# Chunked attention with memory slots feeding a Snake MLP: V loads with their edge rows, x blocks by crossbar, and loads moved between phases

## The chip, the cores and the metric

The kernel runs on one core of a Trainium2 chip. The metric is device time in microseconds (us) of one execution. A core has TensorE (PE, matmuls), VectorE (DVE), ScalarE (ACT), GpSimd (POOL) and SyncE (SP), each with an instruction stream of its own that runs in the order of the program. GpSimd and SyncE here mostly issue DMA transfers. "Idle before" of an instruction is the time in which its engine stood still just before it.

## The reference

Four batches, eight heads, 768 positions, head size 64. Each chunk of 32 queries attends to its own 32 keys, 16 to the left, 8 to the right, and to 8 memory keys. The result, put together over the heads, is the x of an MLP.

```python
for c in range(nc):                                   # chunk = 32
    l_start = max(0, c_start - 16)
    r_end = min(S, c_end + 8)
    k_full = concat([mem_k, k[:, :, l_start:r_end]])
    v_full = concat([mem_v, v[:, :, l_start:r_end]])
    scores = scale * matmul(q_c, k_full^T)
    a = exp(scores - max);  a = a / (sum(a) + 1e-09)
    out[:, :, c_start:c_end] = matmul(a, v_full)
x = out.transpose(0, 2, 1, 3).reshape(3072, 512)
h = x @ w_in                                          # 512 -> 2048
s = sin(alpha * h)
g = h + s * s / (alpha + 1e-09)
return g @ w_out                                      # 2048 -> 512
```

## The kernel before

Queries are taken in 8 blocks of 96 (three chunks). A block meets 128 rows of keys and values: rows 0 to 63 and 72 to 127 are positions from 16 before the block to 8 behind it, rows 64 to 71 the memory slots. Rows that a chunk must not see get a bias of -30000 before the exponential. The values tile `vw` has one more column of ones, which yields the sum for the division.

The order is: attention of batch 0 (arranged by pairs of heads, "units" of a pair and half of the blocks); MLP pass 0; attention of batch 1; pass 1; and so on. A pass has 16 tiles of the hidden width: `half_first` makes h in PSUM, ScalarE the sine, one of three engines the square, VectorE the sum g into `gT`. The second product (`second`) of a pass is fed in slices into the phases that follow it, and its output is copied to `o_sb` (two buffers) and stored by SyncE's queue.

Loads of V for a batch: the rows of the block itself in two transfers, the edge rows from the neighbours in two more. In batch 0 the edges come first for all heads, then four pairs of heads.

```python
def load_v(b, parts=((0, H),)):
    vw = vws[b % 2][:].rearrange("p h j c -> p (h j) c")
    vf = v[b].rearrange("h (j t) d -> t (h j) d", t=QW)
    n = H * NJ
    if len(parts) > 1:
        load_v_edges(vw, vf, n)
    for h0, h1 in parts:
        c0, c1 = h0 * NJ, h1 * NJ
        nc.gpsimd.dma_start(vw[16:64, c0:c1, 0:D], vf[0:48, c0:c1])
        nc.gpsimd.dma_start(vw[72:120, c0:c1, 0:D], vf[48:96, c0:c1])
    if len(parts) == 1:
        load_v_edges(vw, vf, n)

def put_memv(b, eng, h0, h1): ...    # memory values of batch 0: one VectorE copy
def send_memv(b):                    # of the others: 8 small transfers
    for j in range(NJ):
        nc.sync.dma_start(vws[b % 2][64:72, :, j, 0:D], memv_st[64:72, b])
```

Batches 2 and 3 get k and q as rows (`load_rows`, GpSimd's queue) and turn them by the crossbar, a DMA that transposes, issued by SyncE:

```python
def cross_steps(b):
    for j in range(NJ):
        nc.sync.dma_start_transpose(kTs[b % 2][:, :, P * j:P * j + P], kst[:, j, :])
        yield
    for t in range(NSUB):
        nc.sync.dma_start_transpose(qTs[b % 2][:, :, P * t:P * t + P], qst[:, t, :])
        yield
```

The attention of batches 1 to 3. A value block `x_blk` (96 queries x 512) reaches xT either by crossbar (`j < crossed`) or by four TensorE transposes and a VectorE copy (`turn_x`):

```python
for s in range(NJ + lag + 1):
    if s < NJ:
        ptl[s] = scores(b, s)
    stream.take(n // 2)              # slices of the second product
    if s >= beside_from:
        next(beside, None)           # a crossbar step of the next batch
    j = s - lag
    if j == NJ:
        ahead(1, 0, xT)              # first half of the MLP's tile 1
    if 0 <= j < NJ:
        xbl[j] = values(b, j, ptl.pop(j))
        if j < crossed:
            nc.sync.dma_start_transpose(xT[:, :, QW * j:QW * j + QW], xbl.pop(j)...)
    stream.take(n - n // 2)
    if j == NJ - 1:
        ahead(0, 0, xT)
    if crossed <= j - 1 < NJ:
        turn_x(xT, j - 1, xbl.pop(j - 1))
```

Attention of batch 0 (`turn_k`, `turn_q`: six transposes of a pair and the copies; `sc`: scores of a pair and two exponentials; `pv`: values of a unit, with a reciprocal and a multiply on VectorE; `x`: turn of a unit and a ScalarE copy; `warm(n)`: n matmuls on zeros that keep TensorE busy):

```python
turn_k(0); warm(2); turn_q(0)
...                                  # memory keys
put_memk(0); warm(3); turn_k(1); warm(2); sc(0); turn_q(1)
alphas()
put_memv(0, nc.vector, 0, H)
warm(2); turn_k(2); warm(2); sc(1); turn_q(2); turn_k(3)
warm(4); turn_q(3); sc(2); warm(2); sc(3)
nc.scalar.preload_act_table(ACTF.Sin)
send_memv(1)
plan(big=(4, 0, 2), one=(6, 7))      # PSUM banks of the next steps
units = [(hp, half) for hp in range(HP - 1) for half in range(2)]
pv(0, 0)
for n in range(1, len(units)):
    warm(1); pv(*units[n]); warm(1); x(*units[n - 1])
warm(1)
pv(3, 0); x(2, 1); pv(3, 1); x(3, 0)
ahead(0, 0, xT); ahead(1, 0, xT); x(3, 1); ahead(2, 0, xT)
```

The passes after the first:

```python
load_rows(2)
crossings = cross_steps(2)
xT = attention(1, feed, (6, 8, 4, 4, 4, 3, 3, 3, 3, 1, 1), 2, 0, crossings, 3)   # 0: none crossed
load_v(2)
send_memv(2)
for i in range(1, B):
    last = i == B - 1
    if i > 1:
        crossings = cross_steps(i + 1) if not last else iter(())
    def begin(ft, i=i):
        if ft == (2 if i > 1 else 0):
            for _ in crossings:
                pass
    if i == 1:
        layer(i, xT, "VAVAVAVAAVAAVAVA", begin, 0)      # the engine of each square
        ...
    else:
        layer(i, xT, "AAAV", begin, feed.left() - (0 if last else 16))
    if not last:
        if i + 2 < B:
            load_rows(i + 2)
        ...
        xT = attention(i + 1, feed, (4, 8, 4, 4, 3, 3, 3, 3, 4, 4, 4), 2, 5 if i == B - 2 else 0)
        if i + 2 < B:
            load_v(i + 2)
            send_memv(i + 2)
```

Of the kernel before, what the change touches and what calls it, by code (L numbers as in the profile page):

```python
# [10 lines left out]
QW = 96  # L11
# [31 lines left out]
def kernel(  # L43
# [12 lines left out]
    nc = tc.nc  # L56
    B, H, S, D = q.shape
# [3 lines left out]
    NJ = S // QW  # L61
    HP = H // 2
# [69 lines left out]
        qb = qkst.tile([P, H, 6, D], BF, name="q_bf")  # L132
        return kb, qb

    def load_rows(b):
        for j in range(NJ):
            lo = QW * j - 16
            r0 = max(0, -lo)
            nc.gpsimd.dma_start(  # L139
                kst[r0:64, j, :].rearrange("p (h d) -> p h d", d=D),  # L140
                k[b, :, lo + r0:lo + 64, :].rearrange("h p d -> p h d"),
            )
            n = min(56, S - (QW * j + 48))
            nc.gpsimd.dma_start(  # L144
                kst[72:72 + n, j, :].rearrange("p (h d) -> p h d", d=D),
                k[b, :, QW * j + 48:QW * j + 48 + n, :].rearrange("h p d -> p h d"),
            )
        nc.sync.dma_start(
            kst[64:72], memk_st[64:72, b - 2, :].unsqueeze(1).to_broadcast([NM, NJ, H * D])
        )  # L150
        for t in range(NSUB):
            nc.gpsimd.dma_start(  # L152
                qst[:, t, :].rearrange("p (h d) -> p h d", d=D),
                q[b, :, P * t:P * t + P, :].rearrange("h p d -> p h d"),
            )
# [15 lines left out]

    def load_v(b, parts=((0, H),)):
        vw = vws[b % 2][:].rearrange("p h j c -> p (h j) c")
        vf = v[b].rearrange("h (j t) d -> t (h j) d", t=QW)
        n = H * NJ
        if len(parts) > 1:
            load_v_edges(vw, vf, n)
        for h0, h1 in parts:
            c0, c1 = h0 * NJ, h1 * NJ
            nc.gpsimd.dma_start(vw[16:64, c0:c1, 0:D], vf[0:48, c0:c1])  # L180
            nc.gpsimd.dma_start(vw[72:120, c0:c1, 0:D], vf[48:96, c0:c1])
        if len(parts) == 1:
            load_v_edges(vw, vf, n)

    def load_v_edges(vw, vf, n):
        nc.gpsimd.dma_start(vw[0:16, 1:n, 0:D], vf[80:96, 0:n - 1])
        nc.gpsimd.dma_start(vw[120:128, 0:n - 1, 0:D], vf[0:8, 1:n])

    def put_memv(b, eng, h0, h1):
        eng.tensor_copy(  # L190
            vws[b % 2][64:72, h0:h1, :, 0:D],
            memv_st[64:72, b, h0:h1, :].unsqueeze(2).to_broadcast([NM, h1 - h0, NJ, D]),
        )

    def send_memv(b):
        for j in range(NJ):
            nc.sync.dma_start(vws[b % 2][64:72, :, j, 0:D], memv_st[64:72, b])
# [122 lines left out]
    def warm(n):  # L320
        z = ps[:, rings["one"][0], :]
        for _ in range(n):
            nc.tensor.matmul(z, idle[:, 0:P], idle[:])  # L323
# [55 lines left out]
    def attention_first(kq, alphas, ahead):  # L379
        xT = xp.tile([P, KT, S], BF, name="xT")  # L380
        pt, xb = {}, {}

        def turn_k(hp):
            t = turn(kq[0], hp, None)
            put_k(0, hp, t)
            put_k_edges(0, hp, t)

        def turn_q(hp):
            put_q(0, hp, turn(kq[1], hp, None))

        def sc(hp):
            for half in range(2):
                pt[hp, half] = unit_scores(hp, half)

        def pv(*u):
            xb[u] = unit_values(*u, pt[u])

        def x(*u):
            unit_turn(xT, *u, xb.pop(u))

        turn_k(0)
        warm(2)
        turn_q(0)
        mt = packed(single(), HP, 32)
        for g in range(HP):
            nc.tensor.transpose(mt[:, g, :], memk_bf[0:32, 2 * g:2 * g + 2, :].rearrange("p e d -> p (e d)"), ident[0:32, 0:32])
        nc.vector.tensor_copy(memkT[:], mt)
        put_memk(0)
        warm(3)
        turn_k(1)  # L410
        warm(2)
        sc(0)
        turn_q(1)
        alphas()
        put_memv(0, nc.vector, 0, H)
        warm(2)
        turn_k(2)
        warm(2)
        sc(1)
        turn_q(2)  # L420
        turn_k(3)
        warm(4)
        turn_q(3)
        sc(2)
        warm(2)
        sc(3)
        nc.scalar.preload_act_table(ACTF.Sin)
        send_memv(1)
        plan(big=(4, 0, 2), one=(6, 7))
        units = [(hp, half) for hp in range(HP - 1) for half in range(2)]  # L430
        pv(0, 0)
        for n in range(1, len(units)):
            warm(1)
            pv(*units[n])
            warm(1)
            x(*units[n - 1])
        warm(1)
        pv(3, 0)
        x(2, 1)
        pv(3, 1)  # L440
        x(3, 0)
        ahead(0, 0, xT)
        ahead(1, 0, xT)
        x(3, 1)
        ahead(2, 0, xT)
        return xT
# [73 lines left out]
    def second(i, gT, cut=0):  # L520

        def begin_o():
            bank = take_bank("one")
            kept.add(bank)
            return bank

        def part(s, bank, f0, f1):
            for ft in range(f0, f1):
                nc.tensor.matmul(  # L529
                    ps[:, bank, :], gT[:, ft, P * s:P * s + P], w_out_sb[:, ft, :],  # L530
                    start=(ft == 0), stop=(ft == FT - 1),
                )
                if ft < FT - 1:
                    yield

        def end_o(s, bank):
            kept.remove(bank)
            rings["one"].remove(bank)
            rings["one"].append(bank)
            o_sb = mlp.tile([P, d_model], F32, name="o_sb", bufs=2)  # L540
            if s % 2 == 0 and not state["attending"]:
                nc.vector.tensor_copy(o_sb[:], ps[:, bank, :])  # L542
            else:
                nc.scalar.copy(o_sb[:], ps[:, bank, :])  # L544
            nc.sync.dma_start(out[S * i + P * s:S * i + P * s + P, :], o_sb[:])

        early = []
        if cut:
            for s in range(2):
                early.append(begin_o())  # L550
                yield from part(s, early[s], 0, cut)
        for s in range(NSUB):
            bank = early[s] if s < len(early) else begin_o()
            yield from part(s, bank, cut if s < len(early) else 0, FT)
            end_o(s, bank)
            yield
# [15 lines left out]
        nc.vector.memset(vw[96:128, H - 1, NJ - 1, 0:D], 0.0)  # L572
    load_qk(0, kq, 0, 2)
    masks.make_identity(nc, ident[:])
    for hp in range(1, HP):
        load_qk(0, kq, 2 * hp, 2 * hp + 2)
    load_v(0, [(2 * hp, 2 * hp + 2) for hp in range(HP)])
    nc.gpsimd.dma_start(memv_st[64:72, 1:B].rearrange("n b h d -> n (b h) d"),
                        mem_v[1:B].rearrange("b h n d -> n (b h) d"))
    for kT in kTs:  # L580
        nc.vector.memset(kT[:, :, 0:16], 0.0)
        nc.vector.memset(kT[:, :, 848:856], 0.0)
# [37 lines left out]
    xT = attention_first(kq, alphas, ahead)  # L620
    for c in range(2):
        load_w_out(c)
    kq1 = alloc_qk()
    load_qk(1, kq1, 0, H)
    for bb in range(2):
# [29 lines left out]
    def begin_0(ft):  # L655
        if ft == 3:
            plan(h=[6] + rings["big"])
        if ft == 11:
            load_v(1)
        if ft == 15:  # L660
            prs.extend(pair_up(kq1[0], n) for n in range(3))

# [15 lines left out]
        feed.take(2)  # L678
    nc.scalar.preload_act_table(ACTF.Exp)
    feed.take(4)  # L680
    load_rows(2)
    crossings = cross_steps(2)
    xT = attention(1, feed, (6, 8, 4, 4, 4, 3, 3, 3, 3, 1, 1), 2, 0, crossings, 3)
    load_v(2)
    send_memv(2)

    for i in range(1, B):
        last = i == B - 1
        if i > 1:
            crossings = cross_steps(i + 1) if not last else iter(())  # L690

        def begin(ft, i=i):
            if ft == (2 if i > 1 else 0):
                for _ in crossings:
                    pass

        if i == 1:
            assert feed.left() == 16
            plan(h=[min(rings["one"])] + rings["big"])
            layer(i, xT, "VAVAVAVAAVAAVAVA", begin, 0)  # L700
            free = rings["h"]
            plan(one=(free[0], free[0] + 1), h=free[1:])
        else:
            plan(h=rings["big"])
            layer(i, xT, "AAAV", begin, feed.left() - (0 if last else 16))
        if not last:
            if i + 2 < B:
                load_rows(i + 2)
            plan(big=rings["h"])
            nc.scalar.preload_act_table(ACTF.Exp)  # L710
            feed.take(6)
            xT = attention(i + 1, feed, (4, 8, 4, 4, 3, 3, 3, 3, 4, 4, 4), 2, 5 if i == B - 2 else 0)
            if i + 2 < B:
                load_v(i + 2)
                send_memv(i + 2)
    feed.take(200)


# [28 lines left out]
```

The softmax here doesn't subtract the row's maximum and nothing guards it: scores larger than these inputs give would overflow.

## Time and profile before

| | |
|---|---|
| time, median of 3 runs | 226.51 us (226.2 to 227.45) |
| profiled span | 226.2 us |
| granted clock of TensorE | full throughout |
| loads on GpSimd's queue | 71520 packets, 14.81 MB |
| transfers on SyncE's queue | 23032 packets, 10.88 MB |
| matmul of the first MLP product, 128x384 | 512 of them, 326 ns each |
| matmul of the second, 128x512 | 362 in the trace (a few records are missing), 379 ns each |

The durations of matmuls overlap: eight of the first product follow each other in 1.30 us. The profile's page gives busy time by engine, the span in 40 slices (a digit is tenths of the slice), the chain of work that ended last, and groups of instructions by line. L483 is the first product, L529 the second, L503 the sine, L510 and L507 the squares, L513 the sum g, L270 the scores, L296 the values, L313 and L316 the turn of x and its copy, L542 and L544 the output copies, L545 the store, L159 and L162 the crossbar steps of k and q, L467 that of x.

### The profile page before, as it was taken

Reading aid. Unit: us, or ns where it says so; the run is one execution under the profiler, and the core shown is the slowest. Engines: PE = TensorE matmul, PEld = TensorE weight load, DVE = VectorE, ACT = ScalarE, POOL = GpSimd, SP = SyncE. Lnnn points to the kernel's source line nnn. Section 1 sums busy time; section 2 is a strip of 40 time slices with the busy share of each in tenths; the row PEclk is TensorE's granted clock in tenths of the full one; section 3 lists DMA queues with packets and bytes.
Section 4 is the critical chain, followed back from the end, with each engine's and each line's share of the span. In section 5 each row is a group of like instructions: output and inputs, shape, how many; then the busy total and the mean of one; then the engine's idle time right before and its main releaser. Section 6 shows DMA issues by size and latency. Waiting matters only on the chain.

```text
span 226.2 us, 4432 instructions
## 1 busy us (share of the span) xinstructions
PE 212.5 (94%) x1694; PEld 115.9 (51%) x1720; DVE 132.9 (59%) x234; ACT 152.6 (67%) x226; POOL 84.4 (37%) x106
## 2 busy tenths in 40 slices
PE   7998999999998999999999999978999999999992
PEld 2555555555545655554665555534565555544440
DVE  5684748793516769994763875626653773771110
ACT  2558478894787589999756879777939678651011
POOL 8967843796989941185780000000000000000000
PEclk9999999999999999999999999999999999999999
DMA  5999999999999999999999954542330110111211
GB/s 81 174 121 127 157 210 207 206 204 142 103 216 159 142 112 167 117 135 121 151 180 95 96 95 93 96 139 93 73 110 0 49 46 0 48 48 49 93 65 74
DMA packets 94573, 25.97 MB, mean 115 GB/s; under 512 B 82632, under 2 KB 91480, under 8 KB 94552
## 3 DMA queue, kind: packets, MB, share of 16 engines
q0 software_dynamic: 71520, 14.81, 111.5%
q1 hardware_dynamic: 23032, 10.88, 24.5%
q8 instruction: 13, 0.21, 0.5%
q14 instruction: 8, 0.07, 0.1%
HBM read 29.67 MB, written 6.29 MB: 159 GB/s over the span
## 4 chain that ended last, share of the span: by engine, by line
PE 50%; DVE 7%; ACT 4%; SPq 3%; issue 3%; DMA 1%; DVEq 0%; ACTq 0%
PE ps L529 26%; PE ps L483 18%; DVE gT L513 5%; SPq L162 3%; PE ps L296 2%; PE ps L270 2%; DVE u L510 2%; ACT u L503 2%; PE ps L313 1%; ACT u L507 1%; DMA out_dram<-o_sb 1%; ACT o_sb L544 1%; ACT pt L283 0%; DVE o_sb L542 0%; DVEq L513 0%
## 5 line engine op out<-in xcount | busy, mean ns | idle before, releaser
L529 PE MATMUL ps<-w_out_sb,gT 128*128 128x512 bf16 x362 | 94.7, 379 | 1.5 <-ACT o_sb L544 0.4
L483 PE MATMUL ps<-xT,w_in_sb 128*128 128x384 bf16 x512 | 91.2, 326 | 1.6 <-DVE gT L513 1.2
L513 DVE SCALAR_TENSOR_TENSOR gT<-u,inv_alpha,ps 128x768 bf16<-128x768 f32 x64 | 63.3, 1011 | 24.0 <-ACT u L507 20.0
L483 PEld LDWEIGHTS <-w_in_sb 128*128 128x128 bf16 x512 | 49.6, 98 | 39.0 <-issue 3.4
L503 ACT ACTIVATE u<-ps,alpha_sb 128x768 f32<-128x768 f32 x64 | 56.7, 896 | 18.4 <-PE ps L483 17.5
L529 PEld LDWEIGHTS <-gT 128*128 128x128 bf16 x384 | 34.3, 98 | 30.9 <-issue 0.9
L507 ACT ACTIVATE u<-u 128x768 f32<-128x768 f32 x40 | 33.7, 843 | 1.2
L283 ACT ACTIVATE pt<-ps,biasm 128x256 bf16<-128x256 f32 x72 | 28.6, 481 | 6.7 <-PE ps L270 3.2
L544 ACT COPY o_sb<-ps 128x512 f32<-128x512 f32 x16 | 9.4, 589 | 25.5 <-PE ps L529 25.5
L510 DVE TENSOR_TENSOR u<-u 128x768 f32<-128x768 f32 x18 | 17.1, 953 | 6.0 <-ACT u L503 6.0
L542 DVE COPY o_sb<-ps 128x512 f32<-128x512 f32 x8 | 5.5, 690 | 21.8 <-PE ps L529 17.2
L303 DVE TENSOR_TENSOR x_blk<-ps,rinv 96x512 bf16<-96x512 f32 x24 | 16.5, 686 | 0.8
L144 POOL DMA_DIRECT2D kst<-in_k_dram x16 | 11.6, 725 | 8.8 <-DMA vw<-in_v_dram 4.1
L302 DVE RECIPROCAL rinv<-ps 96x8 f32<-96x8 f32 x24 | 4.9, 202 | 17.0 <-ACT pt L283 10.7
L139 POOL DMA_DIRECT2D kst<-in_k_dram x16 | 11.0, 689 | 8.6 <-DMA vw<-in_v_dram 6.2
L323 PE MATMUL ps<-idle 128*128 128x512 bf16 x35 | 12.5, 448 | 1.5 <-DVE vw L571 1.2
L249 ACT COPY kT<-ps 128x672 bf16<-128x672 bf16 x8 | 5.8, 719 | 9.5 <-PE ps L234 6.7
L296 PEld LDWEIGHTS <-pt 128*128 128x128 bf16 x192 | 9.0, 98 | 4.6 <-issue 0.7
L510 POOL TENSOR_TENSOR u<-u 128x768 f32<-128x768 f32 x6 | 8.9, 1495 | 6.1 <-ACT u L503 6.1
L152 POOL DMA_DIRECT2D qst<-in_q_dram x12 | 10.6, 899 | 1.2 <-DMA kst<-in_k_dram 1.2
L270 PE MATMUL ps<-qT,kT 64*128 64x96 bf16 x192 | 8.3, 205 | 2.6 <-DVE gT L513 2.3
L296 PE MATMUL ps<-vw,pt 128*128 128x65 bf16 x192 | 9.8, 193 | 0.4 <-issue 0.3
(77 smaller groups left out, 150.8 us busy)
## 6 DMA issues: line engine op xcount, KB each, us to landing
out_dram<-o_sb SPq DMA_DIRECT2D x24, 256.0 KB
vw<-in_v_dram POOLq DMA_DIRECT2D x6, 384.0 KB, 14.9
w_out_sb<-in_moe_w_out_dram POOLq DMA_DIRECT2D x2, 1024.0 KB, 18.8
w_in_sb<-in_moe_w_in_dram POOLq DMA_DIRECT2D x3, 512.0 KB, 10.1
qst<-in_q_dram POOLq DMA_DIRECT2D x12, 128.0 KB, 7.0
kst<-in_k_dram POOLq DMA_DIRECT2D x14, 64.0 KB, 6.7
kst<-in_k_dram POOLq DMA_DIRECT2D x14, 56.0 KB, 6.4
k_bf<-in_k_dram POOLq DMA_DIRECT2D x4, 192.0 KB, 4.7
```

Source lines behind the costliest of these rows:

```text
L270: nc.tensor.matmul(sc[:, e, QW * hp:QW * hp + QW], kTs[b % 2][64 * e:64 * e + 64, hp, pitch * j:pitch * j + P], qTs[b % 2][64 * e:64 * e + ...
L283: nc.scalar.activation(pt[:, 0:H * QW].rearrange("p (g e c) -> p g e c", g=2, e=4)[:, :, :, 32 * m:32 * m + 32], sc[:, :, 0:4 * QW].rearra ...
L296: nc.tensor.matmul(otv[:, e, hp, :], pt[:, QW * i:QW * i + P], vws[b % 2][:, 2 * hp + e, j, 0:D + 1],)
L303: nc.vector.tensor_tensor(out=x_blk[:].rearrange("p g e d -> p e g d"), in0=otv[0:QW, :, :, 0:D], in1=rinv[:].unsqueeze(3).to_broadcast([Q ...
L323: nc.tensor.matmul(z, idle[:, 0:P], idle[:])
L483: nc.tensor.matmul(hT[:, hf, 0:HALF], w_in_sb[:, kt, P * ft:P * ft + P], xT[:, kt, HALF * hf:HALF * hf + HALF], start=(kt == 0), stop=(kt ...
L503: nc.scalar.activation(u[:], hT[:, :, 0:HALF], ACTF.Sin, scale=alpha_sb[:, ft:ft + 1])
L507: nc.scalar.activation(u[:], u[:], ACTF.Square)
L510: eng.tensor_tensor(out=u[:], in0=u[:], in1=u[:], op=ALU.mult)
L513: nc.vector.scalar_tensor_tensor(out=gT[:, ft, :].rearrange("p (e c) -> p e c", e=2), in0=u[:], scalar=inv_alpha[:, ft:ft + 1], in1=hT[:, ...
L529: nc.tensor.matmul(ps[:, bank, :], gT[:, ft, P * s:P * s + P], w_out_sb[:, ft, :], start=(ft == 0), stop=(ft == FT - 1),)
L544: nc.scalar.copy(o_sb[:], ps[:, bank, :])
```

## The change

V of a block comes in two transfers that hold the edge rows: rows 0 to 63 start 16 positions ahead of the block, rows 72 to 127 run 8 beyond it. What a block takes from the neighbouring head at an end is masked by the bias as before. In batch 0 the transfers of pair 0 are issued right behind k and q of pair 1, and the two units of pair 0 are done amid the scores. In the attentions of batches 1 and 2 five value blocks go by crossbar, as they did in batch 3 only. The crossbar steps of batch 2's k and q move from the attention of batch 1 to pass 1, those of batch 3 are spread over pass 2, one per tile. Row loads of batch 3 move from behind pass 1 to ahead of pass 2, V of batch 3 to pass 1, and the memory values of batches 1 and 2 to pass 0. Squares of pass 1 go to three engines instead of two, and the output copies during an attention all to VectorE.

```diff
@@ load_v (load_v_edges is gone)
+        flat = v.rearrange("b h s d -> (b h s) d")
+        def part(p0, p1, first, c0, c1):
+            r0 = S * H * b + QW * c0 + first
+            nc.gpsimd.dma_start(
+                vw[p0:p1, c0:c1, 0:D],
+                flat[r0:r0 + QW * (c1 - c0)].rearrange("(n t) d -> t n d", t=QW)[0:p1 - p0],
+            )
         for h0, h1 in parts:
             c0, c1 = h0 * NJ, h1 * NJ
+            if b == 0 and h0 == 0:
+                part(16, 64, 0, 0, 1)
+                c0 = 1
+            part(0, 64, -16, c0, c1)
...
+            part(72, 128, 48, c0, c1)
...
@@ attention_first
         turn_k(1)
+        put_memv(0, nc.vector, 0, H)
         warm(2)
         sc(0)
         turn_q(1)
         alphas()
-        put_memv(0, nc.vector, 0, H)
-        warm(2)
+        warm(3)
+        sc(1)
+        pv(0, 0)
+        warm(1)
+        pv(0, 1)
         turn_k(2)
         warm(2)
-        sc(1)
+        x(0, 0)
         turn_q(2)
+        warm(2)
+        x(0, 1)
         turn_k(3)
-        warm(4)
+        warm(1)
+        sc(2)
         turn_q(3)
-        sc(2)
-        warm(2)
+        warm(3)
         sc(3)
         nc.scalar.preload_act_table(ACTF.Sin)
-        send_memv(1)
...
-        units = [(hp, half) for hp in range(HP - 1) for half in range(2)]
-        pv(0, 0)
+        units = [(hp, half) for hp in range(1, HP - 1) for half in range(2)]
+        pv(1, 0)
@@ second
-            if s % 2 == 0 and not state["attending"]:
+            if s % 2 == 0 or state["attending"]:
                 nc.vector.tensor_copy(o_sb[:], ps[:, bank, :])
@@ loads at the start
-    for hp in range(1, HP):
-        load_qk(0, kq, 2 * hp, 2 * hp + 2)
-    load_v(0, [(2 * hp, 2 * hp + 2) for hp in range(HP)])
-    nc.gpsimd.dma_start(memv_st...)              # now behind the loads of w_out
+    load_qk(0, kq, 2, 4)
+    load_v(0, ((0, 2),))
+    load_qk(0, kq, 4, 6)
+    load_qk(0, kq, 6, 8)
+    load_v(0, ((2, 4), (4, 6), (6, 8)))
@@ pass 0
         if ft == 11:
             load_v(1)
+            send_memv(1)
+            send_memv(2)
@@ from batch 1 on
-    load_rows(2)
+    load_k_rows(2)
+    xT = attention(1, feed, (6, 8, 4, 4, 4, 3, 3, 3, 3, 1, 1), 2, 5)
+    load_q_rows(2)
+    load_v(2)
+
     crossings = cross_steps(2)
-    xT = attention(1, feed, (6, 8, 4, 4, 4, 3, 3, 3, 3, 1, 1), 2, 0, crossings, 3)
-    load_v(2)
-    send_memv(2)
...
         def begin(ft, i=i):
-            if ft == (2 if i > 1 else 0):
+            if i == 1:
                 for _ in crossings:
                     pass
+                if ft == 13:
+                    load_v(3)
+            elif i == 2:
+                next(crossings, None)
 
         if i == 1:
-            layer(i, xT, "VAVAVAVAAVAAVAVA", begin, 0)
+            layer(i, xT, "VAVAAVPAAVPAPVAA", begin, 0)
...
+            if i == 2:
+                load_k_rows(3)
+                load_q_rows(3)
+                crossings = cross_steps(3)
             layer(i, xT, "AAAV", begin, feed.left() - (0 if last else 16))
...
-            if i + 2 < B:
-                load_rows(i + 2)
...
-            xT = attention(i + 1, feed, (4, 8, 4, 4, 3, 3, 3, 3, 4, 4, 4), 2, 5 if i == B - 2 else 0)
-            if i + 2 < B:
-                load_v(i + 2)
-                send_memv(i + 2)
+            xT = attention(i + 1, feed, (4, 8, 4, 4, 3, 3, 3, 3, 4, 4, 4), 2, 5)
+            if i == 1:
+                send_memv(3)
```

## The prediction

> **What bounds the kernel now.** I read the page first (busy shares, the 40 slices), then a table of busy time by stage, then the chain of waits inside the two stages that lose most, then groups and DMA landings.
>
> From the page, busy time and the 40 slices:
>
> ```profile
> PE 212.5 (94%) x1694; PEld 115.9 (51%) x1720; DVE 132.9 (59%) x234; ACT 152.6 (67%) x226; POOL 84.4 (37%) x106
> ...
> PE   7998999999998999999999999978999999999992
> DMA  5999999999999999999999954542330110111211
> ```
>
> TensorE works 94% of the span, so a large gain is not to be had: it has to come out of its 13.7 us of idle time or out of the matmuls it is given. Some 1.2 us of the idle time lie at the start and 4.1 at the end (21.46 busy of the 25.60 from 200.6 us on), where nothing is changed. The DMA engines are loaded in the first 23 slices, up to 130 us.
>
> Busy time by stage (columns: stretch, its length, then busy us and instructions of each engine):
>
> ```profile
> 5.64:19.50 13.86, 13.33 (x196) 7.01 (x198) 8.42 (x27) 8.24 (x12) 10.66 (x14) 1.00 2.51 144
> 19.50:28.40 8.90, 7.90 (x114) 5.22 (x116) 6.78 (x16) 5.33 (x9) 7.92 (x11) 1.00 1.78 146
> ...
> 62.00:79.00 17.00, 15.98 (x201) 9.46 (x203) 9.25 (x24) 12.64 (x29) 15.78 (x21) 1.00 1.91 172
> 79.00:102.50 23.50, 22.30 (x134) 12.40 (x134) 20.72 (x23) 21.68 (x26) 9.42 (x14) 1.00 2.29 132
> 102.50:119.00 16.50, 15.78 (x198) 9.53 (x201) 9.93 (x25) 12.34 (x29) 11.95 (x14) 1.00 2.43 151
> ...
> 138.00:153.20 15.20, 13.05 (x80) 6.82 (x82) 7.70 (x9) 11.53 (x16) 0.00 (x0) 1.00 0.52 114
> ```
>
> In order: scores of batch 0, its values, attention of batch 1, MLP pass 1, attention of batch 2, end of MLP pass 2. Pass 1 is the only stage where VectorE (20.72) and ScalarE (21.68) are nearly as full as TensorE; the end of pass 2 is the only one after the start and before the tail with over 2 us of TensorE idle. The chain of waits in these two, 79 to 103 us and 136 to 154 us:
>
> ```profile
> by line: DVE gT L513 30.1%; PE ps L483 21.1%; DVE u L510 18.7%; issue 12.9%; ACT u L503 11.3%; ACT u L507 3.6%; PE ps L270 1.4%; PE ps L529 1.3%; DVEq L513 0.4%
> ```
>
> ```profile
> 147.82 1.22 SPq L162
> ...
> 149.13 2.23 DMA out_dram<-o_sb
> ...
> 151.44 0.69 DVE o_sb L542
> 152.14 0.93 DVE gT L513
> ...
> 153.11 0.35 PE ps L270 x8
> ```
>
> Pass 1 is paced by VectorE (49% of its chain). Pass 2 ends in a queue: 14 crossbar transposes stand in a row on SyncE's queue from 128.97 to 149.03, the output stores wait behind them, VectorE waits 4.60 us for an output buffer, gT comes late, and the scores wait 2.05 us for the bank.
>
> **What the Trainium skill says.** "DMA: Bandwidth & Descriptors", DMA Transpose (X-bar): a plain transpose is issued by SyncE or ScalarE only. So here the transposes share SyncE's order with stores and memory values, as the chain above shows. The same page, Queues, rings and completion order: each DMA engine takes turns between its queues by packets. The trace agrees that they share: the seven transposes of k rows stand on SyncE's queue from 70.93 to 82.95, 1.72 us each, against 1.20 (median) for the five of x blocks (96 rows rather than 128) from 157 us on, when no GpSimd load runs. "GPSIMD Engine Reference", Engine selection, puts a two-input elementwise operation at about twice VectorE's time; here the square takes 1495 ns on GpSimd and 953 on VectorE, 1.6 times. "TensorE: Matmul & The Clock Gate", Measured speedup vs the span model, says matmuls run strictly in order; so TensorE pays in full when the half of x that comes next isn't there.
>
> **The change part by part.**
>
> Start. The V loads of pair 0 are issued at 9.28 and 10.01 now and land 9.4 us later, at 19.4; the first values matmul waits for them at 19.57. Behind q1 (lands 4.11 + 4.4 = 8.5) they should land about 11 (estimate: 120 rows x 16 blocks = 1920 packets, at the rate at which all 7656 V packets of the batch land now between 13.5 and 23.6, 2.5 us). q and k of pairs 2 and 3 come some 2.5 us later, at 12.6 to 16, and aren't needed before. Two of eight values units move into the score stage. After them the phase of values is six units of 0.20 + 0.69 us on VectorE, spaced 0.91 (eight took 20.01 to 27.33). But the score stage grows. Replaying TensorE's order with its durations (idle-filling matmul 0.21, turn of six 0.45, scores of a pair 1.40, x turn 0.18): sc(1) runs to about 13.0, pv(0,1) must wait for the second exponential (14.1) that frees its bank and ends at 14.4, and what follows up to sc(3) is 4 x 0.45 + 8 x 0.21 + 2 x 0.18 + 2 x 1.40 = 6.6: end at 21.1, against 19.34 now. Then 21.5 + 6 x 0.91 = 27.0 against 27.33. **Gain 0.3 us**, not 1.8: what was idle-filling work was partly cover for ScalarE's exponentials.
>
> Five x blocks by crossbar, in batches 1 and 2. Each saves four transposes on TensorE, 0.17 us in the chain where they are packed, and a 0.35 us copy on VectorE. 2 x 5 x 0.17 = **1.7 us**.
>
> Output copies in attention all to VectorE. ScalarE's late copies stopped TensorE for 0.61 us at 70.4 and 0.38 at 111.4 (a transpose and a matmul of the second product waiting for a bank). VectorE has room: 9.25 of 17.00 busy, and five copies less. **Gain 1.0 us**.
>
> Squares of pass 1: seven on VectorE and nine on ScalarE become five, eight, and three on GpSimd. VectorE: 16 x 1.01 + 7 x 0.95 = 22.8 becomes 20.9. ScalarE: 16 x 0.90 + 9 x 0.84 = 22.0 becomes 21.1. TensorE needs 128 x 0.162 = 20.8. The three come level, so not all of 1.9 is won: **1.3 us**.
>
> Transposes of batch 3 one per tile of pass 2 rather than in two blocks. A tile lasts 1.95 us and a transpose 1.3, so the queue of SyncE drains and stores slip in. The 2.05 us wait goes, with 0.2 of smaller ones around it: **2.2 us**. Row loads of batch 3 go behind V, and GpSimd has 20 us for them.
>
> The memory values of batches 1 and 2 go to pass 0 (16 issues of 0.8 to 1.1 us, as now, 45 to 61 us), when SyncE has nothing else, and are off the path. V in two loads of 64 and 56 rows rather than four has the same bytes.
>
> On the other side: crossing x costs latency where loads run. At 62 to 79 and 98 to 115 us GpSimd's queue is full, and a transpose at 1.7 us per 1.3 us step falls behind: five blocks lag by about 2 us plus landing, while the first MLP matmuls of a pass come some 5 us after block 3's values. I allow **0.5 us for each of the two stages**.
>
> Sum: 0.3 + 1.7 + 1.0 + 1.3 + 2.2 - 1.0 = 5.5; 226.5 - 5.5 = 221.0 us.
>
> **The rivals.**
> One: crossing under load becomes the wait. For it: 1.72 against 1.20 us, and TensorE can't go round. Against it: at 158 us crossing has five steps of slack, and SyncE has less else to do in attention after the change (k rows go to pass 1). If each block took 3 us, the half of x would be 3 to 4 us late in both batches: 225 to 228.
> Two: GpSimd's squares stand behind the loads of V. For it: GpSimd waited 5.02 and 4.05 us for V landings in pass 1, and its order is kept. Against it: those waits stood before row loads of batch 3, which move to pass 2; what stands ahead of the first square issues without waiting now (75.37 to 79.6), and the first square comes some 8 us into the pass. If it happened, the 1.3 would be lost and 1 or 2 more: 222 to 224.
> Three: the start gets slower. If ScalarE's table load and exponentials push the last values to 28.5, 1.2 us go: 222.5.
> Four: pass 1 becomes TensorE's and the queue stays clear, without late x: 219.
>
> **Range and chances.** The five gains stand on waits that the trace shows; their sum without the allowance is 6.5 (220.0), with the second or third rival 222 to 224, with the first 225 or more. Range 218.4 to 224.3. 2% is 222.0, 1.0 above my number: faster by over 2% 0.63, within 2% 0.32, slower 0.05 (only the first rival in both batches).
>
> **What would show it.** First values matmul near 13.5 and the last VectorE multiply of batch 0 near 27; no VectorE output copy waiting for a store, and no hole at 147 to 153 (shifted); pass 1 from 23.5 to about 22 us with GpSimd squares of 1.5 us; attention of batches 1 and 2 about 1 us shorter each, without waits of the MLP's first matmul for a crossing of x. It is wrong if that matmul waits for x over 1 us, if GpSimd's squares start later than ScalarE's sine by more than 1 us, or if V of batch 2 lands after its first values matmul.

## The result, and the profile after

The changed kernel takes 234.97 us (median of 4 runs, 234.33 to 235.41) against 226.35 for the kernel before on the same chip: a ratio of 1.037, with a 95% interval of 1.0326 to 1.0415. It is 3.7% slower. The prediction was 221.0, with a range up to 224.3.

The head of the page and three rows of the 40 slices, kernel after:

```profile
span 233.4 us, 4347 instructions
...
PE 212.5 (91%) x1652; PEld 114.3 (49%) x1678; DVE 135.2 (58%) x231; ACT 147.5 (63%) x216; POOL 86.6 (37%) x103
...
PE   7989899989999098999994999999999999999993
PEclk9999999999999859999999999999999999999999
DMA  6999999999999999549999995553321101102212
```

TensorE has 42 instructions fewer and the same busy time: matmuls at a lower clock have eaten what was saved. There are two new holes: slice 14 (75.9 to 81.7 us, digit 0), in which the granted clock falls to 8, and to 5 in the slice behind it; and slice 22 (digit 4), where the clock stays full. Both are named by one row of the waits (total us, times, longest), and both stand at the first matmul of an MLP pass in the timeline of TensorE (start, us, what; in brackets the idle time before it and its releaser), kernel after. The second profile of the kernel before, shown last, has no such wait:

```profile
PE ps L498 <- DMA xT<-x_blk: 9.3, 2, 5.9
```

```profile
75.21 0.38 PE L544 MATMUL ps<-w_out_sb,gT 128*128 128x512 bf16 x1
81.47 1.44 PE L498 MATMUL ps<-xT,w_in_sb 128*128 128x384 bf16 x4 [5.88 <-DMA xT<-x_blk]
...
85.05 4.88 PE L498 MATMUL ps<-xT,w_in_sb 128*128 128x384 bf16 x24
...
125.89 0.81 PE L498 MATMUL ps<-xT,w_in_sb 128*128 128x384 bf16 x4 [3.38 <-DMA xT<-x_blk]
```

```profile
76.41 0.81 PE L483 MATMUL ps<-xT,w_in_sb 128*128 128x384 bf16 x4
```

(L498 is the first product of the MLP, L483 in the kernel before; L544 the second, before L529; L513 is now L528.) The wait is for the crossed x blocks. The first matmul of a pass reads half of x, blocks 0 to 3. The chain of waits, 60 to 95 us, and SyncE's timeline, kernel after, show for how long block 3 was under way:

```profile
73.15 8.18 DMA xT<-x_blk
81.33 0.14 issue
81.47 1.44 PE ps L498 x4
```

```profile
73.15 2.94 SPq L482 DMA_TRANSPOSE xT<-x_blk  x2
```

SyncE begins to issue the crossbar transpose of block 3 (96 rows) at 73.15 us; an issue takes some 1.3 us here. The data is there 8.18 us after that start. This time, from the start of the issue until the data is there, is called the landing below. In batch 2 the landing of block 3 takes 7.17 us (118.59 on).

The rest of the loss is found by dividing the span at the same events in each kernel. The table gives the length of each stage in us, from the starts in the timelines (the last row runs to the end of the last first product); "before, again" is a second profile of the unchanged kernel, for a reason that comes below, and "no crossing" is the changed kernel without the crossing in batches 1 and 2 (an experiment).

| stage | before, again | after | no crossing |
|---|---|---|---|
| start to first product of pass 0 | 26.64 | 26.71 | 26.71 |
| to its second product at the end | 22.51 | 23.09 | 22.99 |
| to first scores of batch 1 | 12.11 | 12.12 | 12.11 |
| attention of batch 1 | 15.15 | 19.55 | 14.64 |
| MLP pass 1 | 24.57 | 27.16 | 25.01 |
| attention of batch 2 | 15.29 | 17.26 | 15.44 |
| MLP pass 2 | 33.40 | 33.42 | 33.42 |
| attention of batch 3 | 13.94 | 13.72 | 13.73 |
| pass 3 to the last tile | 34.72 | 34.69 | 34.68 |

After against no crossing: 4.91 + 2.15 + 1.82 = 8.88 of the 8.9 us between their spans (233.4 and 224.5). So the loss lies in three stages and hangs on the five x blocks.

### The profile page after: what moved, and what is told of

Read it like the earlier page. It is cut to its first block, busy times and chain, and to the rows that moved or that the text cites. A ratio compares the mean times of both kernels' runs of the same rounds, so it can differ in the third digit from the quotient of the medians.

```text
span 233.4 us, 4347 instructions
## 1 busy us (share of the span) xinstructions
PE 212.5 (91%) x1652; PEld 114.3 (49%) x1678; DVE 135.2 (58%) x231; ACT 147.5 (63%) x216; POOL 86.6 (37%) x103
## 4 chain that ended last, share of the span: by engine, by line
PE 69%; DVE 11%; DMA 7%; ACT 6%; issue 5%; POOL 1%; DVEq 0%; ACTq 0%; POOLq 0%
PE ps L544 33%; PE ps L498 26%; DMA xT<-x_blk 7%; DVE gT L528 4%; ACT u L518 3%; PE ps L280 3%; DVE u L525 2%; PE ps L306 2%; DVE qT L266 1%; PE ps L333 1%; PE ps L241 1%; PE ps L244 1%; ACT u L522 1%; PE ps L323 1%; DVE x_blk L372 1%
## 5 line engine op out<-in xcount | busy, mean ns | idle before, releaser
L498 PE MATMUL ps<-xT,w_in_sb 128*128 128x384 bf16 x512 | 93.1, 331 | 10.6 <-DMA xT<-x_blk 9.3
L544 PE MATMUL ps<-w_out_sb,gT 128*128 128x512 bf16 x362 | 94.7, 380 | 2.2 <-DVE gT L528 1.3
L528 DVE SCALAR_TENSOR_TENSOR gT<-u,inv_alpha,ps 128x768 bf16<-128x768 f32 x64 | 63.3, 1012 | 23.8 <-ACT u L522 19.6
L498 PEld LDWEIGHTS <-w_in_sb 128*128 128x128 bf16 x512 | 50.1, 99 | 49.2 <-issue 14.5
L544 PEld LDWEIGHTS <-gT 128*128 128x128 bf16 x384 | 34.4, 98 | 32.5 <-issue 2.1
L522 ACT ACTIVATE u<-u 128x768 f32<-128x768 f32 x39 | 32.9, 843 | 1.2
L557 DVE COPY o_sb<-ps 128x512 f32<-128x512 f32 x17 | 11.7, 689 | 26.9 <-PE ps L544 25.4
L525 POOL TENSOR_TENSOR u<-u 128x768 f32<-128x768 f32 x9 | 13.4, 1501 | 29.9 <-ACT u L518 29.9
L525 DVE TENSOR_TENSOR u<-u 128x768 f32<-128x768 f32 x16 | 16.1, 1004 | 6.8 <-ACT u L518 6.8
L180 POOL DMA_DIRECT2D vw<-in_v_dram x15 | 18.2, 1223 | 0.0
L559 ACT COPY o_sb<-ps 128x512 f32<-128x512 f32 x7 | 4.1, 584 | 19.0 <-PE ps L544 19.0
L333 PE MATMUL ps<-idle 128*128 128x512 bf16 x33 | 11.4, 445 | 1.5 <-DVE vw L586 1.2
L280 PEld LDWEIGHTS <-kT 64*128 64x128 bf16 x192 | 4.8, 94 | 10.2 <-issue 10.2
```

What stands on the lines that cost most here:

```text
L180: nc.gpsimd.dma_start(vw[p0:p1, c0:c1, 0:D], flat[r0:r0 + QW * (c1 - c0)].rearrange("(n t) d -> t n d", t=QW)[0:p1 - p0],)
L280: nc.tensor.matmul(sc[:, e, QW * hp:QW * hp + QW], kTs[b % 2][64 * e:64 * e + 64, hp, pitch * j:pitch * j + P], qTs[b % 2][64 * e:64 * e + ...
L498: nc.tensor.matmul(hT[:, hf, 0:HALF], w_in_sb[:, kt, P * ft:P * ft + P], xT[:, kt, HALF * hf:HALF * hf + HALF], start=(kt == 0), stop=(kt ...
L522: nc.scalar.activation(u[:], u[:], ACTF.Square)
L525: eng.tensor_tensor(out=u[:], in0=u[:], in1=u[:], op=ALU.mult)
L528: nc.vector.scalar_tensor_tensor(out=gT[:, ft, :].rearrange("p (e c) -> p e c", e=2), in0=u[:], scalar=inv_alpha[:, ft:ft + 1], in1=hT[:, ...
```

## The experiments

The leading theory, L: crossing x is late because the transposes share the DMA engines with the loads that GpSimd has in flight then (k and q rows and V of the next batch). Its rival, S: it is late because SyncE's queue also carries output stores, so that a transpose stands behind or beside them. A third question was whether the 2.15 us of pass 1 are a clock lowered by the idle time, or the changed split of squares. No kernel here leaves out any of the computation; a few add a little to it.

### Without the crossing in batches 1 and 2

```diff
-    xT = attention(1, feed, (6, 8, 4, ...), 2, 5)
+    xT = attention(1, feed, (6, 8, 4, ...), 2, 0)
-            xT = attention(i + 1, feed, (...), 2, 5)
+            xT = attention(i + 1, feed, (...), 2, 5 if i == B - 2 else 0)
```

> The changed kernel with one part undone: no x block of batches 1 and 2 goes by crossbar, all are turned on TensorE. Theory L and theory S both say that the crossings cost the stall of the first MLP matmul (5.88 and 3.38 us) and, behind the first of them, about 2.5 us of slowed clock; without them these 11.8 us go, the 2 x 0.85 us of saved transposes come back: about 224.5 us, ratio 0.985 to 0.995 to the kernel before. Theory C (the loss is in other parts, the crossing wait only shows it): above 230 us.

Measured: 226.75 us, ratio 1.0009 (0.9995 to 1.0024). The timeline of TensorE, no crossing:

```profile
76.45 0.81 PE L498 MATMUL ps<-xT,w_in_sb 128*128 128x384 bf16 x4
...
86.17 13.39 PE L498 MATMUL ps<-xT,w_in_sb 128*128 128x384 bf16 x80 [0.15 <-DVE gT L528]
...
100.07 1.46 PE L544 MATMUL ps<-w_out_sb,gT 128*128 128x512 bf16 x6 [0.51 <-DVE gT L528]
...
112.00 0.38 PE L544 MATMUL ps<-w_out_sb,gT 128*128 128x512 bf16 x1 [0.80 <-DVE o_sb L557]
```

The first matmul of the pass waits for nothing. The whole loss is the crossing of these two batches; and all the other parts of the change together, for which the prediction counted 4.8 us, bring nothing that can be measured.

### The loads out of the way, or the stores out of the queue

Loads later: k rows, q rows and V of batch 2 are issued at tile 1 of pass 1, those of batch 3 at tile 1 of pass 2, each held back by a GpSimd square at tile 0; the crossbar steps of k and q follow from tile 2 on. Attention then has crossings and stores but no GpSimd loads.

```diff
-    load_k_rows(2)              # before attention of batch 1
-    load_q_rows(2); load_v(2)   # after it
+                if ft == 1:     # in pass 1; the same for batch 3 in pass 2
+                    load_k_rows(2); load_q_rows(2); load_v(2)
-            layer(i, xT, "VAVAAVPAAVPAPVAA", begin, 0)
+            layer(i, xT, "PAVAAVPAAVPAPVAA", begin, 0)
```

> The changed kernel with crossings kept, but GpSimd's row loads of batch 2 and V of batch 2 held back to pass 1 (behind a GpSimd square of its tile 0), rows and V of batch 3 to pass 2, so that no load runs beside the attentions of batches 1 and 2. Theory L (the loads take the DMA engines' turns): the waits of the first MLP matmul for x, 5.88 and 3.38 us, both fall below 0.5 us, five crossings move in about 7 us, and the clock isn't slowed there. Theory S (output stores in the same queue): they stay at 5 to 6 and 3 to 4 us. The total is not the point, as batch 2's k and q come late for its scores: some 5 to 8 us are lost there.

Stores elsewhere: the output stores of the attention stages go out from ScalarE's queue.

```diff
-            nc.sync.dma_start(out[...], o_sb[:])
+            (nc.scalar if state["attending"] else nc.sync).dma_start(out[...], o_sb[:])
```

> The changed kernel with the output stores of the attentions issued from ScalarE's queue instead of SyncE's, so that only crossings stand in SyncE's. Theory S: waits for x fall from 5.88 and 3.38 us to below 2 and 1, the total to about 226 us. Theory L: the stores still share the engines, waits stay above 4 and 2.5 us, total 231 to 236 us.

Busy time by stage (length, then busy us and instructions of PE, PEld, DVE, ACT, POOL; granted clock; DMA share; GB/s) in the attention of batch 1, first the kernel after, then the one with loads later:

```profile
62.00:76.00 14.00, 13.33 (x168) 6.83 (x171) 7.90 (x19) 11.67 (x26) 13.75 (x18) 1.00 1.90 168
```

```profile
62.00:76.00 14.00, 14.00 (x174) 6.92 (x172) 7.42 (x17) 11.99 (x27) 0.00 (x0) 1.00 0.27 81
```

Timeline of TensorE and chain of waits, loads later:

```profile
76.34 0.81 PE L498 MATMUL ps<-xT,w_in_sb 128*128 128x384 bf16 x4 [0.24 <-DMA xT<-x_blk]
...
130.90 0.81 PE L498 MATMUL ps<-xT,w_in_sb 128*128 128x384 bf16 x4
```

```profile
73.89 2.31 DMA xT<-x_blk
```

Timeline of TensorE, stores elsewhere:

```profile
80.15 1.44 PE L498 MATMUL ps<-xT,w_in_sb 128*128 128x384 bf16 x4 [4.72 <-DMA xT<-x_blk]
...
128.38 1.44 PE L498 MATMUL ps<-xT,w_in_sb 128*128 128x384 bf16 x4 [3.76 <-DMA xT<-x_blk]
```

Without GpSimd's loads (POOL busy 0.00 in place of 13.75, DMA share 0.27 in place of 1.90) the same step takes 2.31 us in place of 8.18, and the waits of 5.88 and 3.38 us become 0.24 and none. With the stores gone from the queue, all five transposes issue in one row (7.56 us from 67.70), and the waits are still 4.72 and 3.76. L stands. S alone does not make the wait: with loads later the stores are still in SyncE's queue, and the wait is gone. Moving them took 1.2 us off one wait and nothing off the other; that is no clean measure of S, since the k transposes of batch 2 then start right behind x, at 75.36 us in place of 86.13. What L leaves open is whether the bytes, the number of small packets or the sharing inside the DMA engines is at fault: rows and V were moved together.

Both kernels are slower as wholes than the changed one, for other reasons than x: loads later takes 250.19 us (1.1041, 1.0987 to 1.1095), because the loads that now stand ahead of GpSimd's squares hold them up (gT waits 24.1 us in total for them, 12.86 before one matmul); stores elsewhere takes 242.22 (1.0686, 1.0643 to 1.0728), with the sine on ScalarE standing still twice behind ScalarE's own stores, 12.77 us up to 88.26 and 11.65 up to 135.40. In the chain of waits the first of these stores is held until a k transpose has landed, at 87.80.

### The clock after the idle time

In the wait of batch 1, TensorE gets 27 matmuls on zeros into a bank that is free; nothing reads them.

```diff
+                if b == 1:
+                    spare = next(n for n in rings["one"] if n not in kept)
+                    for _ in range(27):
+                        nc.tensor.matmul(ps[:, spare, :], idle[:, 0:P], idle[:])
```

> The changed kernel with 27 more matmuls on zeros (27 x 0.213 = 5.75 us) put into TensorE's order ahead of the first MLP matmul of batch 1, that is into the 5.88 us in which it waits for x. If the stall also costs a slowed clock afterwards (24 matmuls in 4.88 us instead of 4.07, four in 1.44 instead of 0.81), the full clock is kept and 2 to 2.5 us are won: 232.6 us. If the slow matmuls come from elsewhere (late x, waits for banks): 235 us as before, or more.

Timeline of TensorE and the row of the granted clock, filled wait:

```profile
76.52 5.99 PE L490 MATMUL ps<-idle 128*128 128x512 bf16 x27 [0.23 <-DVE xT L326]
82.34 0.81 PE L502 MATMUL ps<-xT,w_in_sb 128*128 128x384 bf16 x4
```

```profile
PEclk9999999999999999999999999999999999999999
```

Pass 1 takes 25.01 us, exactly as without the crossing, in place of 27.16: the 2.15 us were the clock that followed the idle time, and not the split of squares. How long an idle stretch must be for this, the runs do not settle. Four matmuls behind the wait take 1.44 us after 5.88 (kernel after) and after 4.72 and 3.76 (stores elsewhere), but 0.81, at full clock, after 3.38 (kernel after) and also after 3.76 in batch 2 of the filled wait. The time is 234.61 us (1.0361, 1.0311 to 1.0412): the total does not show the gain clearly. In this profile the start, which the filling cannot reach, took 0.84 us longer and the two attentions 0.56 more together, which gives most of it back.

### Two blocks in place of five

```diff
-    xT = attention(1, feed, (6, 8, 4, ...), 2, 5)
+    xT = attention(1, feed, (6, 8, 4, ...), 2, 2)
-            xT = attention(i + 1, feed, (...), 2, 5)
+            xT = attention(i + 1, feed, (...), 2, 5 if i == B - 2 else 2)
```

> The changed kernel with two crossed blocks in batches 1 and 2 instead of five (batch 3 keeps five). Theory L with a queue that falls behind (about 2.3 us per block against a step of 1.3 to 1.5): two blocks land some 4 to 5 us after the first is issued, ahead of the first MLP matmul: waits below 0.5 us, and 2 x 2 x 0.17 us of saved transposes: 226.0 us. A theory in which each crossing has a fixed long latency of 8 us (as block 3's): the wait stays at 2 to 4 us, 230 us or more.

Measured: 224.99 us, 0.9952 (0.9933 to 0.9972). The pass begins at 75.86 without a wait; attention of batch 1 takes 14.03 us. Blocks 0 and 1 cross at 67.84 to 71.3 and have over 4 us to land; the later blocks do not. A fixed landing of 8 us is ruled out. The stage is 0.61 us shorter than without the crossing, where 0.34 was expected; why stays open.

### The kernel before, looked at again

The queue at the end of pass 2, for which the prediction counted 2.2 us, stood in one profile only. A second one of the unchanged kernel:

> The kernel before, unchanged, profiled once more: the first profile has a span of 226.2 us, while its runs lie around 224.8 us of span. If the 2.05 us wait of the scores for gT at 153 us belongs to every execution, it is there again and the term of 2.2 us stands; then the missing 2 us of the run without crossings are lost elsewhere. If the first profile caught an unusually long queue, the wait is below 1 us now and the term was too large from the start.

Timeline of TensorE, kernel before, second profile:

```profile
149.67 0.34 PE L270 MATMUL ps<-qT,kT 64*128 64x96 bf16 x8
150.91 0.34 PE L270 MATMUL ps<-qT,kT 64*128 64x96 bf16 x8
```

No wait stands before the scores, where the first profile has one of 2.05 us. Its span is 224.0 us and the first profile's 226.2: the prediction had read an execution that was longer than most. In this one the crossings of q ended at 146.6 in place of 149.0, and four stores followed at once. Most of the 2.2 us was not there to win.

### The squares of pass 1

Old split, without the crossing of x in batches 1 and 2, so that nothing on GpSimd but loads runs in pass 1:

```diff
-            layer(i, xT, "VAVAAVPAAVPAPVAA", begin, 0)
+            layer(i, xT, "VAVAVAVAAVAAVAVA", begin, 0)
```

> The kernel without crossings of batches 1 and 2 and, besides, with the squares of pass 1 as before (seven on VectorE, nine on ScalarE, none on GpSimd). If my term of 1.3 us for the squares holds: 1.3 us longer than without crossings alone, 228.0 us. If what its trace shows is right (0.4 us won in the stream of matmuls, 0.4 lost at the end of the pass, where V loads of batch 3 stand on GpSimd): within 0.5 us of it, 226.8 to 227.3 us.

Timelines of GpSimd and of TensorE, old split:

```profile
85.38 1.72 POOL L180 DMA_DIRECT2D vw<-in_v_dram  x1 [5.04 <-issue]
```

```profile
102.96 0.34 PE L280 MATMUL ps<-qT,kT 64*128 64x96 bf16 x8 [0.68 <-DMA qT<-qst]
...
107.60 0.34 PE L280 MATMUL ps<-qT,kT 64*128 64x96 bf16 x8 [0.77 <-DMA qT<-qst]
```

Of four runs one, 233.5 us, fell in a slower state of the chip and does not count (with it the median is 231.18); the others are 229.39, 229.66 and 232.69, a ratio of 1.0206 (1.0106 to 1.0305). That is 2.9 us more than without the crossing in the medians, and 3.4 in the two profiles (227.9 and 224.5), of which 0.83 lie in the start, ahead of the edit. GpSimd's squares do something that the prediction had not seen: they hold back the loads that follow them in its program. Without them V of batch 3 is all issued by 87.6 us in place of 98.22 to 102.2, its traffic meets the crossings of k and q, and the scores wait for q. The two waits make 1.45 us of the 1.96 by which pass 1 and the attention of batch 2 are longer; the rest stays open. The split itself shows in the stream of 80 first products, 13.78 us here as in the kernel before, 13.39 with the new split. To keep the hold and take two of the three squares off GpSimd:

```diff
-            layer(i, xT, "VAVAAVPAAVPAPVAA", begin, 0)
+            layer(i, xT, "VAVAVAVAAVPAVAVA", begin, 0)
```

> The kernel without crossings of batches 1 and 2, with the squares of pass 1 as before except for one, at tile 10, which stays on GpSimd (seven on VectorE, eight on ScalarE), so that GpSimd's order holds V and rows of batch 3 back as in the run without crossings (226.75 us). If the long time with the old squares (231.2) came from these loads running early beside the crossings of q and k: the waits for q are gone, at most 0.7 us over the run without crossings, 226.8 to 227.5 us. If it came from VectorE and ScalarE having more squares: 229 us or more.

226.68 us, 1.0015 (0.9998 to 1.0033), pass 1 24.94 us against 25.01 with three. As work, two more squares on GpSimd make pass 1 no shorter (0.07 us longer). The one that is left, as a hold for the loads behind it, is worth 3.0 us in the medians (229.66 against 226.68) and 2.5 in the profiles, their starts set apart (ScalarE also has one square less than with the old split).

### Loads placed for the crossings

Batch 1 crosses no x; V of batch 3 goes out at tile 7 of pass 1, and its rows at tile 1 of pass 2 behind a GpSimd square, so that attention of batch 2 has few loads in flight and crosses five blocks; V in four transfers in place of two.

```diff
-            load_v(1)
+            load_v(1, ((0, 4), (4, 8)))      # the same for batches 2 and 3
-                if ft == 13:
-                    load_v(3)
+                if ft == 7:
+                    load_v(3, ((0, 4), (4, 8)))
+                if ft == 1:                  # in pass 2, no longer ahead of it
+                    load_k_rows(3); load_q_rows(3)
+                if ft > 3:
+                    next(crossings, None)    # two at tiles 8 and 12
-            layer(i, xT, "AAAV", ...)
+            layer(i, xT, "PAAVAAAVAAAVAAAV" if i == 2 else "AAAV", ...)
```

> A version meant to keep what theory L allows: no crossings of x in batch 1; five in batch 2, but V of batch 3 loaded at tile 7 of pass 1, when GpSimd's queue is empty in the run without crossings (88 to 99 us), and the rows of batch 3 held back to pass 2 behind a GpSimd square; V of batches 1 to 3 in four transfers rather than two. Theory L: no wait for x in batch 2 (below 0.3 us), 0.85 us of transposes saved against the run without crossings, 0.4 to 0.6 us at the end of passes 0 and 1: 224.8 to 225.5 us. Theory S or a fixed latency: the wait of 3.4 us is there, 228 us or more.

225.27 us, 0.9958 (0.9939 to 0.9978). Attention of batch 2 takes 13.75 us (15.44 without the crossing) and pass 2 begins without a wait for x: five blocks pay once the loads are elsewhere. Timeline of TensorE, relaid loads:

```profile
98.16 2.76 PE L498 MATMUL ps<-xT,w_in_sb 128*128 128x384 bf16 x16 [0.85 <-DVE gT L528]
...
123.61 1.46 PE L498 MATMUL ps<-xT,w_in_sb 128*128 128x384 bf16 x8 [0.61 <-DVE gT L528]
```

These new waits for gT stand behind GpSimd's squares: one of 0.85 after the earlier V load, one of 0.61 after the square put in as a hold. The last pair of kernels takes the hold without the square (a copy of one column, which waits for x), V of batch 3 at tile 11, squares of pass 1 spread otherwise, and two blocks in batch 1; they differ in the engine of attention's output copies alone.

```diff
+                    nc.gpsimd.tensor_copy(gate[:], xT[:, 0, S - 1:S])   # tile 1 of pass 2
                     load_k_rows(3); load_q_rows(3)
+    xT = attention(1, feed, (...), 2, 2)
+            layer(i, xT, "VAPAAVPAAVPAVAVA", begin, 0)     # pass 1
+            layer(i, xT, "AAAV", ...)                      # pass 2
# the second kernel only:
-            if s % 2 == 0 or state["attending"]:
+            if s % 2 == 0 and not state["attending"]:
```

VectorE copies:

> Two crossed blocks in batch 1, five in batch 2 with its loads out of the way: V of batch 3 at tile 11 of pass 1 (GpSimd squares at tiles 2, 6, 10), rows of batch 3 held back by a GpSimd copy of one column of xT instead of a square; V in four transfers. Output copies of the attentions on VectorE as in the changed kernel. Theory L: no waits for x, against the relaid version (225.3) 0.34 us for two blocks, and the waits of 0.85 us and 0.61 us for gT that the GpSimd squares cost there: 223.6 to 224.8 us.

ScalarE copies, as in the kernel before:

> The same as the one before, with the output copies of the attentions on ScalarE, as in the kernel before. My term of 1.0 us for VectorE's copies would make it 1.0 us longer. The trace of the run without crossings shows waits for VectorE's copies too (0.80 us at 112, 0.22 at 79): then the two are within 0.4 us of each other.

223.71 us (0.9881, 0.9851 to 0.9912) and 223.22 us (0.9867, 0.9847 to 0.9888). Both beat the changed kernel, and the kernel before by 1.2 and 1.3%. Timeline of TensorE, and busy time in the attention of batch 2, ScalarE copies:

```profile
75.65 0.81 PE L499 MATMUL ps<-xT,w_in_sb 128*128 128x384 bf16 x4
...
114.32 0.81 PE L499 MATMUL ps<-xT,w_in_sb 128*128 128x384 bf16 x4
```

```profile
104.00:114.00 10.00, 9.79 (x133) 5.33 (x135) 6.51 (x16) 8.97 (x21) 0.00 (x0) 1.00 1.37 134
```

Both passes begin without a wait for x. In batch 2 GpSimd issues nothing where the changed kernel had it issuing loads; in batch 1 it still does (13.60 of 13.60 us busy from 62.0 to 75.6), and there only the two blocks cross that have time to land. Against the second profile of before, attention of batch 1 is 1.12 us shorter, attention of batch 2 0.87 and pass 1 0.32.

## Why the prediction was wrong

Of the 14.0 us between 221.0 and 234.97, 8.9 are the crossing (8.2 lost against the kernel without it, 0.7 forecast as won). The other 5.1 are, within 0.3, the four other gains, 4.8 in all, which came to nothing.

**Crossing x: 1.7 gained less 1.0 allowed.** This is the step that failed. The gain was there, if the wait is set apart: attention of batch 1 grew by 4.91 us with a wait of 5.88, so 0.97 was saved; in batch 2 it is 3.38 - 1.82 = 1.56, of which 0.80 is a wait for an output copy that the kernel without the crossing has. The 0.85 for each batch was well sized. The allowance, "0.5 us for each of the two stages", was not: 5.88 and 3.38 us. It came from "1.72 against 1.20 us", two issue times, and took the space between two issues for the cost of the load. The 1.72 was misread besides: it is the mean of a row of seven, of which six take 1.22 to 1.38 us and the last 3.41. SyncE's timeline, kernel before (the fifth is counted in both lines):

```profile
70.93 7.09 SPq L159 DMA_TRANSPOSE kT<-kst  x5
76.63 6.32 SPq L159 DMA_TRANSPOSE kT<-kst  x3
```

So this row did not show "that they share". The blocks of x in batch 1, too, are issued nearly as fast under load: in 1.305 us in the median of five in the changed kernel, 1.207 with the loads moved. What the load stretches is the landing, 8.18 us against 2.31. The prediction spoke of "about 2 us plus landing" and put no number on the landing. The rest of that sentence held: TensorE was done at 75.59 us, 4.9 after the start of block 3's values (70.68), so at the start of the issue (73.15) 2.4 us were left. A landing of 2.31 would have fitted; one of 8.18 leaves the wait of 5.88. The Trainium skill's "DMA: Bandwidth & Descriptors", Queues, rings and completion order (engines take turns between queues by packets), fits this, but no run here separates that from other ways of sharing. That TensorE "pays in full" held: in the 5.88 us no later matmul ran. (In "TensorE: Matmul & The Clock Gate" the strict order of matmuls stands under The mechanism, not under the heading that the prediction gives.)

**The first rival** had the mechanism and said "3 to 4 us late in both batches: 225 to 228". It was still too small: x came 5.88 and 3.38 us late, and it left out what the idle time does next, 2.15 us of lower clock in pass 1. With both, less the transposes saved, 8.9 us go. Its chance of 0.05 rested on "SyncE has less else to do", which is true and beside the point.

**The queue of pass 2, 2.2.** Read from one execution, in which the wait was 2.05; the second profile of before has none. The hole made the attention of batch 3 16.06 us long in the first profile; it is 13.94 in the second and 13.72 after. So at most 0.2 was to be had in an execution like the second. "Row loads of batch 3 go behind V, and GpSimd has 20 us for them" also went otherwise: nothing holds them, so they are issued from 109.32 on, in the attention of batch 2, where they add to the load on the second crossing.

**Squares of pass 1, 1.3.** Pass 1 takes 25.01 us in place of 24.57 (no crossing against before). The stream of first products is 0.4 us faster (80 matmuls in 13.39 in place of 13.78). By the prediction's own 0.162 us for each, 80 make 13.0, so no more than 0.8 was to be had in it. The end of the pass, with V of batch 3 issued at tile 13 and gT 0.51 late, gives 0.44 back; another 0.39 goes at its start, where TensorE waits for a copy of xT behind an output copy on VectorE (see below). The second rival (squares behind loads) did not come true in this kernel: gT waits for all of GpSimd's squares 2.9 us in eight pieces, 0.7 at most. It did in the kernel with loads later, 24.1 us.

**Output copies, 1.0.** Attention of batch 1 is 0.51 us shorter without the crossing, that of batch 2 0.15 longer, with a wait of 0.80 for the copy on VectorE, that of batch 3 0.21 shorter. The last pair of kernels, which differ in nothing else, puts it at 0.5 us the other way, inside the intervals. Their stages say more, since 0.84 us of the two profiles' difference is the start (27.60 and 26.76 us), where no such copy is made. With VectorE's copies the attentions take 14.03, 14.35 and 13.72 us, with ScalarE's 14.03, 14.42 and 13.94: 0.29 won. Pass 1 takes 24.63 against 24.25: 0.38 lost, at its start. Timeline of TensorE, VectorE copies, then ScalarE copies:

```profile
79.15 3.41 PE L499 MATMUL ps<-xT,w_in_sb 128*128 128x384 bf16 x20 [0.22 <-DVE xT L327]
```

```profile
77.52 4.07 PE L499 MATMUL ps<-xT,w_in_sb 128*128 128x384 bf16 x24
```

Not a gain: what TensorE waits for moved from one engine's copies to the other's.

**The start, 0.3.** 26.71 against 26.64 us, no gain and no loss; the first values matmul at 13.24 us, "near 13.5", and the reason given (the score stage grows as the values stage shrinks) held. Starts varied over the profiles, 26.6 to 26.9 us in eight and 27.5 to 27.7 in five; no run here says why.

**Not in the sum:** the end of pass 0, 0.48 us longer (22.99 against 22.51). "V in two loads of 64 and 56 rows rather than four has the same bytes" held for the bytes only: the two transfers are issued in one row of 3.36 us, and a VectorE square beside it takes 1.55 us. Timeline, kernel after:

```profile
45.14 3.36 POOL L180 DMA_DIRECT2D vw<-in_v_dram  x2
...
47.09 1.55 DVE L525 TENSOR_TENSOR u<-u 128x768 f32<-128x768 f32 x1
```

The stretch is longer by what this square is longer. Over the eight profiles with two transfers it takes 1.12 to 1.55 us and the stretch 22.67 to 23.09. With four it takes 0.95 in the relaid kernel and the first of the last pair (22.51 and 22.50) and 1.19 in the second (22.74). So the slow square accounts for the loss; what slows it stays open.

## What to carry to other kernels

Before work is moved from an engine to a transfer, measure how long the transfer takes to land beside everything in flight at that moment, and compare it with the time to its first reader; issue times do not show it. An instruction that seems to be only work can also be the hold that keeps later loads from starting, so ask what each load of a queue waits for before its neighbours are moved. A wait worth 2 us in one profile is to be seen in a second before it is counted as a gain, and a mean of issue times is to be looked at one by one.

## What the runs showed of the hardware

- A crossbar transpose of 96 rows landed 2.31 us after the start of its issue without GpSimd loads in flight, and 7.17 and 8.18 us after it with them (one block each); the median issue time in batch 1 was 1.207 and 1.305 us.
- One idle stretch of 5.88 us was followed by a lower granted clock (slices of 0.8 and 0.5): 24 matmuls took 4.88 us where 0.167 each, as in the stream of 80, makes 4.0, and the pass lost 2.15 us. A stretch of 3.38 us lowered no slice; of two of 3.76 us, one was followed by slow matmuls and one was not.
- A VectorE square of 0.95 us took 1.12 to 1.55 in eight profiles beside GpSimd's issue of two large transfers, and beside four smaller ones 0.95, 0.95 and 1.19.
- Output stores on ScalarE's queue, with transposes running on SyncE's, went with standstills of ScalarE of 12.77 and 11.65 us; why stays open.
